# Product 1 of the last two chunks by seven half-size products throughout, with some of its activations on VectorE and three stages in a written order

## The chip, the core and the metric

The kernel runs on one core of a Trainium2 chip. The metric is the device time of one execution in microseconds (us). TensorE is called PE here, VectorE DVE, ScalarE ACT, GpSimd POOL, and SP is the engine that issues most DMAs.

## What is computed

Eight attention heads over four sequences of 768 positions, three heads ("retrieval") with a causal mask and five ("streaming") with a window of 64 positions and 4 sink positions, and behind it a two-layer block with a leaky ReLU:

```python
scores = scale * np.matmul(q, k.transpose(0, 1, 3, 2))        # (4, 8, 768, 768), head_dim 64
scores = np.where(mask, scores, -1e9)                         # causal, or window + sinks, by head
a = softmax(scores); attn = np.matmul(a, v)
x = attn.transpose(0, 2, 1, 3).reshape(3072, 512)
h = x @ w_in                                                  # product 1, 512 -> 2048
g = np.maximum(0.01 * h, h)
out = g @ w_out                                               # product 2, 2048 -> 512
```

## The kernel before

The 3072 positions are cut into eight chunks of 384 (`CH`), numbered 0 to 7; a sequence has two. For each chunk the attention gives `xts[n]`, the transposed input of product 1. Product 1 gives `g_all` (features on partitions, 16 tiles of 128 features), and product 2 takes pairs of 128-row tiles of `g_all` and writes rows of the output.

The work is software-pipelined. **Stage n** is the pass of the last loop (L1115 on) with that n: it runs product 1 of chunk n, the attention of chunk n+1 (up to stage 6) and product 2 of chunk n-1. Chunk numbers and stage numbers are the same thing in what follows. Nothing is scheduled by a tool: each engine executes its instructions in the order in which Python calls them, and semaphores hold an instruction until its inputs are there and its output buffer is free. The order is made of lists of small steps ("slots"): `Attention.slots` (a score matmul with its exponential on ACT and mask on DVE, and some slots later the product with V, "AV"), `in_slots` (product 1) and `steps` (product 2, each step half a unit of 4 matmuls of 256 columns, 14 steps for a pair). `merge` spreads one list evenly through another.

**Product 1** has two forms. A *tick* makes one tile of 128 features for the chunk: 4 matmuls of 384 columns into one PSUM bank (tag `ph`, two banks), then one leaky ReLU on ACT into `g_all` (L597, L600). A *quad* (class `Quad`) makes four such tiles by seven half-size products P1 to P7 in place of eight (sums and differences of blocks of the input, `x_sum`, and of the weights, `in_sum`, stand in for blocks). Each product is 4 matmuls of 192 columns (L686). P1, P6, P7 and P4 accumulate in one bank; after P1, P6 and P7 the running total is copied to SBUF by ACT (L700), and the next product may only start when the copy has read the bank. P2, P5 and P3 are added to those copies by DVE (L714), and each result passes the leaky ReLU on ACT (`out`, L693). Before, `BY_SEVEN` gives chunks 4, 6 and 7 two quads (features 0 to 1023) and eight ticks each.

**Product 2** uses the same trick with class `Pair`: units P1 to P7 of 8 matmuls (L800, L779), sums on DVE (L761), copies on ACT (L804) and additions on DVE (L805). Its sums of a pair are put in line by `flush` when all 16 tiles of the chunk are there.

PSUM has eight banks, two for each tag: `ph` and `psS` (scores) and `po` (AV) and `py` (product 2).

Of the kernel before, what the change touches and what calls it, by code (L numbers as in the profile page):

```python
# [11 lines left out]
FP32 = mybir.dt.float32  # L12
# [9 lines left out]
def kernel(  # L22
# [36 lines left out]
    def bank(tag, shape, dtype):  # L59
        return ps.tile(shape, dtype, name=tag, tag=tag, bufs=BANKS[tag])  # L60
# [245 lines left out]
    class Attention:  # L306
        def __init__(self, n, score_tags=("psS",), po_tags=("po", "po", "po", "po"), xt_eng="a", cross=False, xt_tag="psS"):
            self.n = n
            self.b, self.c = ORDER[n]
            self.i = self.b % 2  # L310
            xts[n] = rot.tile([128, 4, CH], BF16, name="xt", tag="xt", bufs=2)
            self.po = {}
            self.tags = score_tags
            self.po_tags = po_tags
            self.sc = 0
            self.xt_eng, self.xt_tag = xt_eng, xt_tag
            self.cross = cross
            self.sink_lo = 128 if self.c == 0 else 0
            self.units = {h: (self.retr(h) if IS_RETR[h] else self.stream(h)) for h in range(H)}
# [261 lines left out]


    done = [0] * NCH
    BY_SEVEN = {4: (0, 1), 6: (0, 1), 7: (0, 1)}

    def slab(n):
        return 4 if n % 2 else n // 2 % 2
# [1 line left out]
    def costing(us, f):  # L589
        f.us = us  # L590
        return f

    def in_slots(n, tags=("ph",)):
        def tick(t, tag=None):
            ph = bank(tag or tags[t % len(tags)], [128, 512], FP32)
            for g in range(KG):
                nc.tensor.matmul(ph[:, 0:CH], lhsT=w_in_bf[:, g, 128 * t : 128 * t + 128],  # L597
                                 rhs=xts[n][:, g, :] if n else xts[0][:, :, g, :], start=(g == 0), stop=(g == KG - 1))
            done[n] += 1
            nc.scalar.activation(out=g_all[:, slab(n) : slab(n) + 3, t, :],  # L600
                                 in_=ph[:, 0:CH].rearrange("p (j t) -> p j t", j=3), func=ACTF.Prelu, alpha=0.01)

        ks = BY_SEVEN.get(n, ())
        ticks = [costing(0.65, lambda t=t: tick(t)) for t in range(NG) if t // 4 not in ks]
        if n + 1 == NCH:
            several = [Quad(n, k, tag).slots() for k, tag in zip(ks, ("psS", "po", "ph"))]
            if len(ks) > 2:
                r = []
                for t in range(12):
                    r += [fs[t - 2 * i] for i, fs in enumerate(several) if 0 <= t - 2 * i < 8]  # L610
                    if t in (0, 1, 9, 10):
                        r.append(ticks.pop(0))
                return r
# [33 lines left out]
    def x_sums(n):  # L647
        x = xts[n].rearrange("p g (j e t) -> p g j e t", j=3, e=2)
        b = lambda a, e: x[:, KH * a : KH * a + KH, :, e, :]
        t = rot.tile([128, 4, KH, 3, 64], BF16, name="x_sum", tag="x_sum", bufs=1)  # L650
        for i, y, z in ((1, b(0, 1), b(0, 0)), (2, b(1, 1), t[:, 0]), (3, b(1, 1), b(0, 1)), (4, b(1, 0), t[:, 1])):
            nc.vector.tensor_tensor(t[:, i - 1], y, z, op=ALU.subtract)
        x_sum[n] = t
        if n + 1 == NCH:
            temps[n] = [rot.tile([128, 2, CH], FP32, name=nm, tag=tag, bufs=bufs) for nm, tag, bufs in
                        (("p1s", "kd", 2), ("us", "kd", 2), ("u3s", "kb", 1))]

    class Quad:


        def __init__(self, n, k, tag):
            self.n, self.k, self.tag = n, k, tag
            self.bank, self.late = {}, []

        def slots(self):
            return [costing(0.33, lambda u=u: self.unit(u)) for u in ("P1", "P6", "P7", "P4", "P2", "P5", "P3")] + [costing(0.0, lambda: self.late.pop()())]

        def unit(self, u):
            n, k = self.n, self.k
            while self.late:  # L670
                self.late.pop()()
# [9 lines left out]
            if first:  # L681
                self.bank[at] = bank(self.tag, [128, 512], FP32)
            s = self.bank[at]
            for m in range(2):
                for g in range(KH):
                    nc.tensor.matmul(s[:, 192 * m : 192 * m + 192], lhsT=lhs[:, g, 128 * m : 128 * m + 128], rhs=rhs[:, g],  # L686
                                     start=first and m == 0 and g == 0, stop=(g == KH - 1), skip_group_check=True)
            self.empty(u, s[:, 0:CH])

        def out(self, src, m, e):  # L690
            t = 4 * self.k + 2 * m
            dst = g_all[:, slab(self.n) : slab(self.n) + 3, t : t + 2, 64 * e : 64 * e + 64]
            nc.scalar.activation(out=dst.rearrange("p j x t -> p x j t"), in_=src.rearrange("p (x j t) -> p x j t", x=2, j=3),  # L693
                                 func=ACTF.Prelu, alpha=0.01)
            self.left -= 1
            if not self.left:
                done[self.n] += 4

        def empty(self, u, s):
            copy = lambda o: nc.scalar.activation(out=o, in_=s, func=ACTF.Copy)  # L700
            if u == "P1":
                self.left = 4
                self.p1, self.u, self.u3 = (t[:, self.k] for t in temps[n]) if n in temps and self.k < 2 else \
                    (rot.tile([128, CH], FP32, name=nm, tag=nm, bufs=1)[:] for nm in ("p1q", "uq", "u3q"))
                copy(self.p1)
            elif u == "P6":
                copy(self.u)
            elif u == "P7":
                copy(self.u3)
            elif u == "P4":  # L710
                self.out(s, 1, 0)
            else:
                t, m, e = {"P2": (self.p1, 0, 0), "P5": (self.u3, 1, 1), "P3": (self.u, 0, 1)}[u]
                nc.vector.tensor_tensor(t, s, t, op=ALU.add)  # L714
                self.late.append(lambda: self.out(t, m, e))

    def in_tile(t0, j, tag="ph", nt=4):
        ph = bank(tag, [128, 4, 128], FP32)
# [393 lines left out]
    assert not any(lists.values())  # L1112
    load_v(4)

    for n in range(2, NCH):  # L1115
        a, extra = [], ()
        if n + 2 < NCH:
# [10 lines left out]
                load_qk(n + 3, "k" if n > 2 else "kq")  # L1128
        if n + 1 < NCH:
            a = Attention(n + 1, cross=True).slots(lag=2 if n > 3 else 3)  # L1130
            a = into(a, extra) if n > 2 else a
        if n == 2:
            a = [(lambda f=f, i=(6, 9, 12, 15).index(j): (f(), in_sums(0, i + 1))) if j in (6, 9, 12, 15) else f for j, f in enumerate(a)]
        ins = in_slots(n)
        if n == 7:
            x_sums(n)
        if n == 3:
# [70 lines left out]
```

## Time and profile before

| | |
|---|---|
| runs, us | 223.74, 223.10, 221.77 (median 223.1) |
| profiled execution, us | 222.32, of which the span from first to last instruction is 220.5 |
| PE busy (matmuls) | 213.3 us, 97% of the span |
| PE weight loads busy | 169.5 us, 77% |
| DVE busy | 144.8 us, 66% |
| ACT busy | 146.8 us, 67% |
| POOL busy | 73.2 us, 33% |
| stage 5 | about 139.6 to 160.2 us of the span |
| stage 6 | about 160.2 to 188.7 us |
| stage 7 | about 188.7 to 204.6 us, then the last two pairs of product 2 to the end |

Rows of the profile name the engine, the line and the tiles (output<-input), how many there are, the busy time and the mean duration of one in ns. In a timeline the first two columns are start and duration in us. Matmuls overlap in the pipeline, so that the time a group of matmuls takes from the engine is the distance to the start of the next group, not the duration in its own row.

### The profile page before, as it was taken

Reading aid. Unit: us, or ns where it says so; the run is one execution under the profiler, and the core shown is the slowest. Engines: PE = TensorE matmul, PEld = TensorE weight load, DVE = VectorE, ACT = ScalarE, POOL = GpSimd, SP = SyncE. Lnnn points to the kernel's source line nnn. Section 1 sums busy time; section 2 is a strip of 40 time slices with the busy share of each in tenths; the row PEclk is TensorE's granted clock in tenths of the full one; section 3 lists DMA queues with packets and bytes.
Section 4 is the critical chain, followed back from the end, with each engine's and each line's share of the span. In section 5 each row is a group of like instructions: output and inputs, shape, how many; then the busy total and the mean of one; then the engine's idle time right before and its main releaser. Section 6 shows DMA issues by size and latency. Waiting matters only on the chain.

```text
span 220.5 us, 6066 instructions
## 1 busy us (share of the span) xinstructions
PE 213.3 (97%) x2436; PEld 169.5 (77%) x2436; DVE 144.8 (66%) x394; ACT 146.8 (67%) x335; POOL 73.2 (33%) x91
## 2 busy tenths in 40 slices
PE   8898999999899999999999999999999999999993
PEld 5577876668698676886688888777787888888893
DVE  6692597885989785857257875655373846626663
ACT  4767975772466997477768796687478886577220
POOL 8978472049607805305447401800000000000000
PEclk9999999999999999999999999999999999999999
DMA  9999999999999999999999994997320231200222
GB/s 130 154 173 169 188 207 188 179 153 124 152 146 230 175 135 146 155 212 117 145 206 153 139 205 99 157 137 107 81 98 5 62 86 21 95 3 0 95 109 86
DMA packets 112604, 28.79 MB, mean 131 GB/s; under 512 B 102208, under 2 KB 109632, under 8 KB 112576
## 3 DMA queue, kind: packets, MB, share of 16 engines
q0 software_dynamic: 78080, 13.37, 82.5%
q1 hardware_dynamic: 33152, 14.53, 36.2%
q10 hardware_dynamic: 1344, 0.50, 1.0%
q8 instruction: 19, 0.31, 0.7%
q14 instruction: 9, 0.07, 0.1%
HBM read 27.30 MB, written 6.29 MB: 152 GB/s over the span
## 4 chain that ended last, share of the span: by engine, by line
PE 85%; POOL 5%; DMA 4%; DVE 3%; ACT 2%; issue 1%; POOLq 0%
PE ph L597 26%; PE py L800 20%; PE po L326 7%; PE py L779 6%; PE psS L357 5%; PE ph L686 4%; DMA w_in_bf<-in_moe_w_in_dram 4%; PE psS L392 3%; PE psS L597 2%; PE po L779 2%; PE po L800 2%; POOL va L123 1%; POOL qb L116 1%; PE po L686 1%; PE psS L686 1%; ACT at L362 1%
## 5 line engine op out<-in xcount | busy, mean ns | idle before, releaser
L597 PE MATMUL ph<-xt,w_in_bf 128*128 128x384 bf16 x352 | 68.5, 326 | 0.0
L600 ACT ACTIVATE g_all<-ph 128x384 bf16<-128x384 f32 x88 | 43.2, 491 | 21.0 <-PE ph L597 18.3
L597 PEld LDWEIGHTS <-w_in_bf 128*128 128x128 bf16 x384 | 34.1, 97 | 17.3 <-issue 0.5
L362 ACT ACTIVATE at<-psS 128x384 bf16<-128x384 f32 x73 | 35.3, 495 | 8.8 <-PE psS L357 6.1
L800 PEld LDWEIGHTS <-sum 128*128 128x128 bf16 x256 | 23.8, 98 | 4.1
L116 POOL DMA_DIRECT2D kb<-in_k_dram x21 | 18.7, 911 | 20.6 <-DMA kd<-kb 18.6
L123 POOL DMA_DIRECT2D va<-in_v_dram x24 | 21.6, 920 | 0.5 <-issue 0.5
L357 PE MATMUL psS<-qd,kt 128*128 128x384 bf16 (+2 forms) x81 | 20.5, 290 | 0.1
L800 PEld LDWEIGHTS <-g_all 128*128 128x128 bf16 x192 | 18.0, 98 | 2.3
L116 POOL DMA_DIRECT2D qb<-in_q_dram x21 | 18.6, 907 | 2.7 <-DMA w_out_bf<-in_moe_w_out_dram 1.3
L326 PE MATMUL po<-va,at 128*128 128x65 bf16 x219 | 18.7, 194 | 0.0
L326 PEld LDWEIGHTS <-at 128*128 128x128 bf16 x234 | 14.7, 98 | 4.0 <-issue 0.5
L800 PE MATMUL py<-w_sum,sum 128*128 128x256 bf16 x120 | 17.7, 272 | 0.0
L397 ACT ACTIVATE ats<-psS 128x384 bf16<-128x384 f32 x33 | 15.7, 490 | 2.6 <-PE psS L392 2.0
L401 DVE TENSOR_TENSOR ats<-ats,m_win 128x384 bf16<-128x384 bf16 x35 | 12.3, 356 | 7.7 <-ACT ats L397 7.3
L761 DVE TENSOR_TENSOR sum<-g_all 128x1024 bf16<-128x1024 bf16 x24 | 16.4, 683 | 0.0
L800 PE MATMUL py<-w_out_bf,g_all 128*128 128x256 bf16 x112 | 16.1, 273 | 0.0
L800 PE MATMUL py<-w_out_bf,sum 128*128 128x256 bf16 x120 | 15.7, 273 | 0.0
L425 DVE TENSOR_TENSOR xs<-po,linv 128x384 bf16<-128x384 f32 x27 | 15.1, 558 | 0.9
L779 PEld LDWEIGHTS <-sum 128*128 128x128 bf16 x152 | 13.2, 98 | 2.2 <-issue 0.5
L264 DVE COPY kt<-kd 64x512 bf16<-64x512 bf16 x36 | 12.9, 366 | 1.3 <-DMA kd<-kb 0.9
L805 DVE TENSOR_TENSOR o<-py,u 128x256 f32<-128x256 f32 x15 | 6.3, 422 | 8.6 <-PE py L800 5.4
(249 smaller groups left out, 415.5 us busy)
## 6 DMA issues: line engine op xcount, KB each, us to landing
out_dram<-o SPq DMA_DIRECT2D x23, 256.0 KB, 3.9
va<-in_v_dram POOLq DMA_DIRECT2D x24, 128.0 KB, 7.2
qb<-in_q_dram POOLq DMA_DIRECT2D x21, 128.0 KB, 6.8
kb<-in_k_dram POOLq DMA_DIRECT2D x21, 128.0 KB, 6.3
w_out_bf<-in_moe_w_out_dram POOLq DMA_DIRECT2D x4, 512.0 KB, 12.0
w_in_bf<-in_moe_w_in_dram POOLq DMA_DIRECT2D x2, 512.0 KB, 8.7
w_in_bf<-in_moe_w_in_dram POOLq DMA_DIRECT2D x4, 256.0 KB, 7.7
vb<-va SPq DMA_DIRECT2D x6, 170.6 KB, 3.4
```

The lines of the kernel that those rows point to most:

```text
L116: nc.gpsimd.dma_start(out=t[:, g], in_=nat[nm][b, c, :, :, g])
L123: nc.gpsimd.dma_start(out=va[b][:, 3 * c + g, :, 0:D], in_=nat["v"][b, c, :, :, g])
L326: nc.tensor.matmul(o, lhsT=lhsT, rhs=rhs, start=first, stop=False, skip_group_check=True)
L357: nc.tensor.matmul(s[:, off : off + w], lhsT=kt[i][hh][:, p, 128 * kj : 128 * kj + 128], rhs=q_of(n, p, lo, CH), start=(j == 0), stop=(j = ...
L362: nc.scalar.activation(out=a[:, 0:off], in_=s[:, 0:off], func=ACTF.Exp, scale=SM)
L397: nc.scalar.activation(out=av_, in_=s[:, 0:CH].rearrange("p (j e f) -> p j e f", j=3, e=2), func=ACTF.Exp, scale=SM)
L425: nc.vector.tensor_tensor(xs[:], po[:, :, :, 0:D], linv.to_broadcast([128, 3, 2, D]), op=ALU.mult)
L597: nc.tensor.matmul(ph[:, 0:CH], lhsT=w_in_bf[:, g, 128 * t : 128 * t + 128], rhs=xts[n][:, g, :] if n else xts[0][:, :, g, :], start=(g == ...
L600: nc.scalar.activation(out=g_all[:, slab(n) : slab(n) + 3, t, :], in_=ph[:, 0:CH].rearrange("p (j t) -> p j t", j=3), func=ACTF.Prelu, alp ...
L761: nc.vector.tensor_tensor(self.s[i], x, y, op=op)
L779: nc.tensor.matmul(s[:, 0 : c1 - c0], lhsT=lhs[:, j, :], rhs=rhs[:, j, c0:c1], start=first and j == 0, stop=(j == NH - 1), skip_group_chec ...
L800: nc.tensor.matmul(s, lhsT=lhs[:, j, :], rhs=rhs[:, j, :], start=u in ("P1", "P2", "P5") and j == 0, stop=(j == NH - 1), skip_group_check= ...
```

## The change

Chunks 6 and 7 get four quads each and no ticks. Stages 5, 6 and 7 no longer merge lists: a string per stage (`WOVEN`) names the list from which each next step is taken: `p` a step of product 2, `a` a slot of attention, `t` a tick, `A` to `D` the steps of the four quads (seven products, then a last one that only puts the outstanding leaky ReLU in line), `x` the four sums of the input, `e` a copy of transposed keys, `I` one of four new weight sums (for features 1024 to 2047), `v` a transfer of shifted values.

In a woven quad the products come in the order P1, P2, P6, P5, P7, P4, P3; P2, P5 and P3 use one bank of another tag (`SIDE`: `ph` in stage 6, `po` in stage 7), and P5 is added after P7 has been copied. The copies of a quad lie in one tile with two halves (`s0` to `s3`), so that P7's copy takes the place of P1's and has to wait for the leaky ReLU that reads it. `OUTS` names, for the 16 leaky ReLUs of each chunk, those that DVE does (`v`: 9 of chunk 6, 5 of chunk 7), each as two `scalar_tensor_tensor` of 192 elements per partition.

```diff
-    BY_SEVEN = {4: (0, 1), 6: (0, 1), 7: (0, 1)}
+    BY_SEVEN = {4: (0, 1), 6: (0, 1, 2, 3), 7: (0, 1, 2, 3)}
+    SIDE = {5: 'po', 6: 'ph', 7: 'po'}
+    OUTS = {6: 'vvavvvaavaavvvaa', 7: 'vaaavaavaaaavaav'}
+    WOVEN = {
+        5: "IptatattapatpaaeetaatepaIpaapttatpattIatvtppppeIeettppp",
+        6: "pxpAaAappAaaAAapApAaBpBBaAaBBaapBpBaapCpCaCaBCpCpaaCpaaCDapaDaDppaaDDpppDDpppCDppppp",
+        7: "pxpBABApCABpABApBApApBBDCCpDCDCADBpDpCDCDCpDppp",
+    }
...
+        if n in WOVEN:
+            return {"t": ticks, **{"ABCD"[j]: Quad(n, k, ("psS" if j < 2 else "ph") if n + 1 == NCH else "ph", True).slots() for j, k in enumerate(ks)}}
...
-        if n + 1 == NCH:
-            temps[n] = [rot.tile([128, 2, CH], FP32, name=nm, tag=tag, bufs=bufs) for nm, tag, bufs in
-                        (("p1s", "kd", 2), ("us", "kd", 2), ("u3s", "kb", 1))]
+        if n in (6, 7) and len(BY_SEVEN[n]) > 0:
+            parts = [rot.tile([128, 2, CH], FP32, name=nm, tag=tag, bufs=bufs) for nm, tag, bufs in
+                     (("s0", "kd", 2), ("s1", "kd", 2), ("s2", "kb", 1), ("s3", "qb", 1))]
+            temps[n] = [[t[:, x] for x in range(2)] for t in parts]
...
+        ORDERS = (("P1", "P6", "P7", "P4", "P2", "P5", "P3"), ("P1", "P2", "P6", "P5", "P7", "P4", "P3"))
...
+            if u == "P5" and self.woven:
+                self.bank[at] = self.bank["a"]
+            elif first:
+                self.bank[at] = bank(SIDE[n] if u == "P2" and self.woven else self.tag, [128, 512], FP32)
...
-            nc.scalar.activation(out=dst.rearrange("p j x t -> p x j t"), in_=src.rearrange("p (x j t) -> p x j t", x=2, j=3),
-                                 func=ACTF.Prelu, alpha=0.01)
+            dst, src = dst.rearrange("p j x t -> p x j t"), src.rearrange("p (x j t) -> p x j t", x=2, j=3)
+            if OUTS.get(self.n, "")[4 * self.k - self.left + 4:][:1] == "v":
+                for x in range(2):
+                    nc.vector.scalar_tensor_tensor(dst[:, x], src[:, x], 0.01, src[:, x], op0=ALU.mult, op1=ALU.max)
+            else:
+                nc.scalar.activation(out=dst, in_=src, func=ACTF.Prelu, alpha=0.01)
...
+    in_sums_left = [lambda i=i: in_sums(1, i + 1) for i in range(4)]
...
+        if n in WOVEN:
+            lists = {"a": a, "p": outs, "x": [lambda: x_sums(n)], "e": [], "v": [lambda: v_shift(n + 2)], **ins}
...
+            for c in WOVEN[n]:
+                lists[c].pop(0)()
```

What this does to the order shows best on DVE and ACT. First DVE at the head of stage 6, before; names are output<-input, `x_sum` and `sum` are the sums for products 1 and 2, `o` rows of the output, `at` and `ats` masked exponentials, `xs` the attention's result:

```order
L652 TENSOR_TENSOR x_sum_3186<-xt_2835,x_sum_3186 128x384
L761 TENSOR_TENSOR sum_3209<-g_all_101 128x1024
L805 TENSOR_TENSOR o_3205<-py_3196,p1_3207 128x256
L367 TENSOR_TENSOR at_3242<-at_3242,m_caus_70 128x128
L365 TENSOR_TENSOR at_3260<-at_3260,m_caus_70 128x2x128
L401 TENSOR_TENSOR ats0_89<-ats0_89,m_win_73 128x3x2x64
L761 TENSOR_TENSOR sum_3332<-g_all_101,sum_3183 128x1024
L423 RECIPROCAL linv_3341<-po_3232 128x6
L425 TENSOR_TENSOR xs_3343<-po_3232,linv_3341 128x384
L714 TENSOR_TENSOR p1q_3224<-ph_3369,p1q_3224 128x384
```

The same place now:

```order
L661 TENSOR_TENSOR x_sum_3196<-xt_2835,x_sum_3196 128x384
L790 TENSOR_TENSOR sum_3213<-g_all_101 128x1024
L728 TENSOR_TENSOR s0_3201<-ph_3225,s0_3201 128x384
L834 TENSOR_TENSOR o_3209<-py_3191,p1_3211 128x256
L719 SCALAR_TENSOR_TENSOR g_all_101<-s0_3201 128x3x64 x2
L367 TENSOR_TENSOR at_3260<-at_3260,m_caus_70 128x128
L728 TENSOR_TENSOR s0_3201<-ph_3225,s0_3201 128x384
L365 TENSOR_TENSOR at_3278<-at_3278,m_caus_70 128x2x128
L719 SCALAR_TENSOR_TENSOR g_all_101<-s0_3201 128x3x64 x2
L728 TENSOR_TENSOR s0_3201<-ph_3225,s0_3201 128x384
L401 TENSOR_TENSOR ats0_89<-ats0_89,m_win_73 128x3x2x64
L728 TENSOR_TENSOR s1_3202<-ph_3330,s1_3202 128x384
```

The first quad's three additions (L728, L714 before) and two of its leaky ReLUs (L719) now stand among the first masks of the stage; before, the first addition of a quad came behind the first `xs`.

Second, ACT in the middle of stage 7, before (L600 a tick's leaky ReLU, L693 leaky ReLUs of quads, L804 copies of product 2):

```order
L693 ACTIVATE g_all_101<-psS_3749 128x2x3x64
L693 ACTIVATE g_all_101<-po_3755 128x2x3x64
L600 ACTIVATE g_all_101<-ph_3822 128x3x128
L804 ACTIVATE u_3832<-py_3727 128x256
L600 ACTIVATE g_all_101<-ph_3846 128x3x128
L693 ACTIVATE g_all_101<-p1s_3724 128x2x3x64 x2
L600 ACTIVATE g_all_101<-ph_3870 128x3x128
L693 ACTIVATE g_all_101<-u3s_3726 128x2x3x64
```

And now, around the place where quad A (copies in `s0`) goes from P7 to P4 (L738 copies and L721 leaky ReLUs of quads, L833 copies of product 2):

```order
L738 ACTIVATE s0_3771<-psS_3791 128x384
L738 ACTIVATE s1_3772<-psS_3785 128x384
L721 ACTIVATE g_all_101<-s0_3771 128x2x3x64
L721 ACTIVATE g_all_101<-psS_3791 128x2x3x64
L833 ACTIVATE u_3872<-py_3760 128x256
L721 ACTIVATE g_all_101<-s1_3772 128x2x3x64
L721 ACTIVATE g_all_101<-psS_3785 128x2x3x64
L738 ACTIVATE s3_3774<-ph_3894 128x384
L721 ACTIVATE g_all_101<-s2_3773 128x2x3x64
```

The ticks' leaky ReLUs that stood between the rows of two quads are gone; rows of four quads (`s0` to `s3`) follow each other, and the first two here free the banks in which quads A and B go on with P4.

More of the change, by code (lines that the diff above doesn't have):

```diff
@@ L680, in unit @@
             first = u in ("P1", "P2", "P5")
-            if first:
-                self.bank[at] = bank(self.tag, [128, 512], FP32)
+            if u == "P5" and self.woven:
+                self.bank[at] = self.bank["a"]
+            elif first:
+                self.bank[at] = bank(SIDE[n] if u == "P2" and self.woven else self.tag, [128, 512], FP32)
             s = self.bank[at]
@@ L697, in out, with add @@
                 done[self.n] += 4
+        def add(self, u, s):
+            t, m, e = {"P2": (self.p1, 0, 0), "P5": (self.u3, 1, 1), "P3": (self.u, 0, 1)}[u]
+            nc.vector.tensor_tensor(t, s, t, op=ALU.add)
+            self.late.append(lambda: self.out(t, m, e))
         def empty(self, u, s):
-            copy = lambda o: nc.scalar.activation(out=o, in_=s, func=ACTF.Copy)
             if u == "P1":
                 self.left = 4
[L703 to L710, printed above, removed]
+                self.p1, self.u, *u3 = temps[n][self.k] if (n := self.n) in temps else \
+                    [rot.tile([128, CH], FP32, name=nm, tag=nm, bufs=1)[:] for nm in self.parts()]
+                self.u3 = u3[0] if u3 else self.p1
+            if u in ("P1", "P6", "P7"):
+                nc.scalar.activation(out={"P1": self.p1, "P6": self.u, "P7": self.u3}[u], in_=s, func=ACTF.Copy)
+            if u == "P4":
                 self.out(s, 1, 0)
[L712 to L715, printed above, removed]
+            elif u == "P7" and self.woven:
+                self.add("P5", self.bank["x"][:, 0:CH])
+            elif u in ("P2", "P3") or u == "P5" and not self.woven:
+                self.add(u, s)
     def in_tile(t0, j, tag="ph", nt=4):
@@ L1130 @@
             a = Attention(n + 1, cross=True).slots(lag=2 if n > 3 else 3)
-            a = into(a, extra) if n > 2 else a
+            a = into(a, extra) if n > 2 and n not in WOVEN else a
         if n == 2:
@@ L1134 @@
         ins = in_slots(n)
+        if n in WOVEN:
+            lists = {"a": a, "p": outs, "x": [lambda: x_sums(n)], "e": [], "v": [lambda: v_shift(n + 2)], **ins}
+            if n > 2:
+                lists["e"] += extra
+            if n == 4:
+                lists["v"] = [lambda: turn_dma(7, "k")]
+            if n in (5, 6):
+                lists["I"] = in_sums_left
+            for c in WOVEN[n]:
+                lists[c].pop(0)()
+            assert not any(lists[c] for c in "aptABCDe" if c in lists) and (n < 6 or not in_sums_left)
+            if n in (3, 4):
+                nc.gpsimd.tensor_copy(hold[0:1, :], xts[n + 1][0:1, 3, 0:1])
+                load_qk(n + 3, "q")
+                load_v(n + 3)
+            outs = [f for k in range(3 * n // 2, 3 * n // 2 + 1 + n % 2) for f in steps(k)]
+            continue
         if n == 7:
```

16 lines of the change are left out of this document (11 added, 5 removed).

## The prediction

> **What bounds the kernel now.** I read the page's totals first, then the busy time by stretches, then the timeline of PE in the stages that change.
>
> ```profile
> span 220.5 us, 6066 instructions
> PE 213.3 (97%) x2436; PEld 169.5 (77%) x2436; DVE 144.8 (66%) x394; ACT 146.8 (67%) x335; POOL 73.2 (33%) x91
> ...
> PEclk9999999999999999999999999999999999999999
> ...
> 139.60:160.20 20.60, 20.60 (x223) 15.27 (x221) 11.01 (x33) 14.10 (x32) 2.77 (x4) 1.00 1.13 119
> ...
> 160.20:188.40 28.20, 28.20 (x339) 23.71 (x338) 17.28 (x44) 21.80 (x51) 0.00 (x0) 1.00 0.18 53
> 188.40:204.30 15.90, 15.90 (x146) 13.21 (x144) 8.06 (x18) 10.97 (x26) 0.00 (x0) 1.00 0.09 34
> ```
>
> The last three rows are stages 5, 6 and 7: length, then busy time of PE, of weight loads, of DVE, ACT and POOL, then the clock. In each, PE's busy time equals the length (20.60 of 20.60, 28.20 of 28.20, 15.90 of 15.90) at full clock. So PE never stands still there, and its matmuls set the time. Two things follow. Time falls only by what PE has less to do; and a new order of steps can win nothing in these stages, it can only lose, by making PE wait.
>
> **What PE saves.** How long a group keeps PE is read from starts, here in stage 7:
>
> ```profile
> 193.08 0.81 PE L597 MATMUL ph<-xt,w_in_bf 128*128 128x384 bf16 x4
> 193.73 0.49 PE L686 MATMUL psS<-x_sum,in_sum 128*128 128x192 bf16 x4
> 194.06 0.49 PE L686 MATMUL po<-x_sum,in_sum 128*128 128x192 bf16 x4
> 194.39 0.81 PE L597 MATMUL ph<-xt,w_in_bf 128*128 128x384 bf16 x4
> 195.04 0.60 PE L800 MATMUL py<-w_sum,sum 128*128 128x256 bf16 x4
> ```
>
> A tick takes 0.65 us (193.08 to 193.73, and 194.39 to 195.04), one product of a quad 0.33 us (193.73 to 194.06 to 194.39). Four ticks are 4 x 0.65 = 2.60; the quad in their place is 7 x 0.33 = 2.31. Each exchange saves 0.29 us; two are made in stage 6 and two in stage 7: **4 x 0.29 = 1.16 us**, 0.58 in each. Stage 5 keeps 16 ticks, 14 steps of product 2 and its attention: 0. What lies ahead of stage 5 and behind stage 7 is untouched. A quad has 28 weight loads against the ticks' 16, so 48 more in all.
>
> ```profile
> 190.07 0.76 PEld L686 LDWEIGHTS <-w_in_bf 128*128 128x128 bf16 x8
> ...
> L686 PEld LDWEIGHTS <-in_sum 128*128 128x128 bf16 x96 | 8.2, 97 | 1.0
> ```
>
> They cost nothing in my sum: one load lasts 97 ns, but stage 6 has 338 of them in 28.20 us, 83 ns apiece on average with three other kinds of matmul between, so loads overlap each other; and the eight products in a row at 190.07 kept their 0.33 us per four.
>
> **What the other engines must then do in time.** The bank of P1, P6, P7, P4 is handed from PE to ACT and back between every two of them. Its price stands in stage 3, where four ticks in a row share two banks:
>
> ```profile
> 106.78 2.85 PE L597 MATMUL ph<-xt,w_in_bf 128*128 128x384 bf16 x16
> 109.47 1.04 PE L800 MATMUL py<-w_out_bf,sum 128*128 128x256 bf16 x8
> ...
> 107.63 0.49 ACT L600 ACTIVATE g_all<-ph 128x384 bf16<-128x384 f32 x1 [0.40 <-PE ph L597]
> ```
>
> The first tick's matmuls are through at 106.78 + 0.65 = 107.43; ACT starts at 107.63, 0.20 later, and takes 0.49. The group needs 2.69 (106.78 to 109.47) and not 2.60: two handovers with 0.65 of other work between cost 0.045 each. So a handover to ACT needs 0.65 + 0.045, about **0.69 us** of other PE work, and nothing is lost above that. For DVE:
>
> ```profile
> 183.57 0.56 DVE L425 TENSOR_TENSOR xs<-po,linv 128x384 bf16<-128x384 f32 x1
> 184.05 0.55 DVE L714 TENSOR_TENSOR p1q<-ph,p1q 128x384 f32<-128x384 f32 x1
> 184.51 0.55 DVE L714 TENSOR_TENSOR u3q<-ph,u3q 128x384 f32<-128x384 f32 x1
> 184.98 0.68 DVE L761 TENSOR_TENSOR sum<-g_all,sum 128x1024 bf16<-128x1024 bf16 x1
> ...
> 184.63 0.53 ACT L693 ACTIVATE g_all<-p1q 128x384 bf16<-128x384 f32 x1
> ```
>
> An addition takes 0.55, so its handover needs about 0.20 + 0.55 + 0.03 = **0.78** (0.03 from its end at 184.60 to the ACT row that waits for it, 184.63). Back to back such operations follow each 0.47 us (184.05 to 184.51 to 184.98).
>
> I counted the PE work between the two ends of each handover in the new strings, with 0.33 for a product, 0.44 for a step of product 2, 0.165 for a score matmul of 384 columns and 0.09 for an AV of three. The shortest: stage 6, quad A, P7 to P4 ("AapA"): 0.165 + 0.09 + 0.44 = 0.69, against 0.69 needed. Stage 7, A's P7 to P4 ("ApBA") and D's P7 to P4 ("DpCD"): 0.44 + 0.33 = 0.77 against 0.69. Stage 6, quad C, P2 to P5 ("CaCaC"): 0.17 + 0.09, 0.33, 0.17 + 0.09, together 0.86 against 0.78. The quads' other handovers have 0.9 or more, but for two of ACT with 0.77 and 0.84. In stage 5 no pair of ticks has less than 0.81. **If ACT and DVE are free at that moment, nothing is lost.** ACT is: it loses 16 leaky ReLUs of ticks, gains 12 copies and 16 leaky ReLUs of quads and gives 14 of all to DVE, 2 fewer in the sum.
>
> DVE is the question. It gets 3 additions for each added quad, and 28 half leaky ReLUs. This operation (two inputs, multiply and maximum, 192 elements of f32) is in no row of before. The nearest:
>
> ```profile
> L974 DVE SCALAR_TENSOR_TENSOR m_one<-diff,m_caus x1: 225/225/225, 1.8 to 1.8; 128x64 bf16<-128x64 bf16 x1
> ...
> L837 DVE TENSOR_TENSOR o<-py,u 128x128 f32<-128x128 f32 x2 | 0.6, 288 | 0.0
> ...
> L805 DVE TENSOR_TENSOR o<-py,u 128x256 f32<-128x256 f32 x15 | 6.3, 422 | 8.6 <-PE py L800 5.4 <-ACT g_all L600 2.6 <-ACT g_all L693 0.7
> ...
> L714 DVE TENSOR_TENSOR p1q<-ph,p1q 128x384 f32<-128x384 f32 x4 | 2.2, 552 | 2.2 <-PE ph L686 2.2
> ...
> L643 DVE TENSOR_TENSOR in_sum<-w_in_bf 128x1024 bf16<-128x1024 bf16 x2 | 1.4, 684 | 0.0
> ```
>
> The same operation on 64 elements took 225 ns, f32 additions of 128, 256 and 384 took 288, 422 and 552. Ends: 0.225 and 0.552. I take the middle between the rows of 128 and 256, 0.355 us, and 0.275 from start to start when back to back (0.08 less, as 0.55 goes to 0.47). Then:
> - Stage 5: four weight sums of 0.684 (L643): 11.01 + 2.74 = 13.75 us in 20.60. Room.
> - Stage 6: 17.28 + 6 x 0.47 + 18 x 0.275 = 25.05 us in 28.20 - 0.58 = 27.62, 91%.
> - Stage 7: 8.06 + 6 x 0.47 + 10 x 0.275 = 13.63 us in 15.90 - 0.58 = 15.32, 89%.
>
> With 0.552 (0.47 back to back) it would be 28.56 in stage 6 and 15.58 in stage 7, more than the stages have; with 0.225, 22.7 and 12.3.
>
> DVE's order is fixed, so a queue nine tenths full is late here and there. I followed DVE's order by hand through both stages with these durations. Where P5 or P3 waits for an addition, or a copy waits for a leaky ReLU that still reads its half tile, the operation was done 0.05 to 0.3 us before PE needed it, at some twelve places by 0.2 or less; none came out late. As twelve so narrow places will not all hold, I charge **0.30 us** (0.025 each), with bounds of 0 and of 3.2 (below).
>
> Moved, and costing nothing: the transfer of shifted values and the DMA transposes of the attention's result still go out some 5.5 us of PE work ahead of the next stage (in stage 5 "tvtpppp" to "ppp" stand behind the last attention slot), as before; stores on SP follow their steps; POOL has nothing in stages 6 and 7 (0.00). If that cover were gone, PE would wait for the transposes at the head of stage 6 or 7.
>
> **Sum.** -1.16 + 0.30 = -0.86 us. The profiled execution took 222.32 us, 220.5 of them span and 1.82 around it: 221.46. The median of the runs is 223.1, 0.78 above that execution: **222.2 us**, 0.4% less.
>
> **Rivals.**
> - *The saving is eaten.* Each of the twelve narrow places is late by 0.1 us, and 1.2 us come back: 223.1. For it: DVE at 91%, and a handover with 0.69 for 0.69. Against it: once PE has waited at one place, the next ones have that much more room.
> - *DVE's leaky ReLUs hold the banks: slower.* In each of the eight quads one addition finds a pair of leaky ReLUs in front of it; the pair takes 0.55, the room is about 0.15, PE loses 0.4 each time: 8 x 0.4 = 3.2 us, net +2.0: 225.1. It decides from the point where such a pair costs more than the room, thus with an operation of 0.552, where DVE has more to do than the stage is long. For it: that end of the bound. Against it: in the new order most additions stand ahead of the pair, and the 64-element row is far below.
> - *The weight loads bind.* If loads went one after another at 97 ns, a quad would take 28 x 0.097 = 2.72 and not 2.31, 0.12 more than the four ticks: 4 x 0.12 = +0.5 us, and with the 0.30 charged above 223.9. Against it: 338 loads in 28.20 us, above.
> - *More than the sum.* There is no idle PE time to win. Only the spread of the runs (221.77 to 223.74) could show it.
>
> The Trainium skill ("Perfetto Trace Analysis", Identifying the Most-Contended Engine) holds that matmul occupancy is a poor measure of how near PE is to its limit and that the share of weight loads should be read with it. By that rule PE's 77% would leave room and fewer columns would not help while more loads might hurt, which is the third rival; the trace here disagrees, since products of 192 columns run at 0.33 us per four and ticks of 384 at 0.65.
>
> That the change does not do what it says can be left aside: the new order has 28 leaky ReLUs on DVE and no tick in stages 6 and 7.
>
> **How the numbers follow.** One per cent, about 2.2 us, is what a measurement of this kernel can tell from no change. Forecast 0.62, eaten 0.20, slower 0.10, loads 0.03, more than the sum or an outlying median 0.05. Faster by over 1% means under 220.9: 0.05. Slower by over 1% means over 225.3: about 0.07, the upper half of the slower rival and a little of the others. Within 1%: 0.88. The forecast itself lies between 221.9 (no stall) and 222.9; with the medians' spread of half a per cent on either side, and reaching to the eaten saving and part of the slower rival, the range is 220.8 to 224.5.
>
> **What would show it.** Right: stages 6 and 7 each about 0.4 to 0.6 us shorter, PE still busy all along, the half leaky ReLU near 0.355, stage 5 as long as before. Wrong: rows in the list of waits where PE waits for DVE (L728) or ACT (L738) by more than 0.3 us in total; a half leaky ReLU above 0.45; PE waiting for transposes at the head of a stage.

## The result, and the profile after

| | before | after |
|---|---|---|
| median of 16 runs each, us | 223.02 (221.77 to 225.82) | 221.38 (220.05 to 222.12) |
| ratio, with its 95% interval | | 0.9924 [0.9898, 0.9949] |
| profiled execution, us | 222.32 | 221.45 |

The change makes the kernel 0.8% faster by this measurement, 1.6 us; run a second time it came out at 0.4% (below). First the totals of the page after, then the row of the half leaky ReLUs (least, median and greatest duration in ns, first and last start):

```profile
span 219.7 us, 6221 instructions
...
PE 212.5 (97%) x2484; PEld 172.8 (79%) x2484; DVE 160.0 (73%) x438; ACT 145.0 (66%) x333; POOL 73.0 (33%) x91
```

```profile
L719 DVE SCALAR_TENSOR_TENSOR g_all<-s x28: 347/352/359, 164.3 to 203.5; 128x192 bf16<-128x192 f32 x28
```

PE has 48 matmuls more and is busy 0.8 us less; DVE is busy 15 us more. The operation that no row of before showed takes 352 ns.

To compare stages I cut both executions at the same instructions: in each stage the first `py<-w_sum,g_all` step of product 2, which opens it. The rows give stage 5, stage 6, stage 7 and the rest: length, then busy time of PE, weight loads, DVE, ACT and POOL (with the number of instructions), the granted clock of PE (1.00 is full), and two columns on DMAs. Before:

```profile
138.91:159.37 20.46, 20.46 (x222) 15.15 (x220) 10.87 (x32) 14.10 (x32) 3.46 (x4) 1.00 1.16 122
159.37:187.84 28.47, 28.47 (x342) 23.95 (x340) 17.55 (x43) 21.80 (x51) 0.00 (x0) 1.00 0.18 53
187.84:203.77 15.93, 15.93 (x146) 13.23 (x144) 8.10 (x17) 10.97 (x26) 0.00 (x0) 1.00 0.09 34
203.77:220.50 16.73, 13.30 (x138) 11.95 (x135) 8.76 (x19) 2.69 (x7) 0.00 (x0) 1.00 0.27 96
```

After:

```profile
139.21:159.86 20.65, 20.63 (x221) 15.20 (x219) 13.32 (x36) 13.60 (x32) 3.46 (x4) 1.00 1.00 116
159.86:187.82 27.96, 27.96 (x365) 25.51 (x363) 24.87 (x68) 20.29 (x49) 0.00 (x0) 1.00 0.20 57
187.82:203.17 15.35, 15.35 (x170) 14.72 (x168) 13.41 (x31) 11.06 (x27) 0.00 (x0) 1.00 0.10 36
203.17:219.70 16.53, 13.31 (x138) 11.95 (x135) 9.25 (x22) 2.80 (x8) 0.00 (x0) 1.00 0.27 96
```

Stage 6 is 0.51 us shorter, stage 7 0.58, stage 5 is 0.19 longer, the rest 0.20 shorter. Stage 5 starts 0.30 later. The sum, 0.30 + 0.19 - 0.51 - 0.58 - 0.20 = -0.80, is the difference of the spans, 220.5 to 219.7.

**Where 0.19 us went in stage 5.** PE looks busy there too (20.63 of 20.65). The loss shows only in the starts, in the timeline after:

```profile
147.47 0.87 ACT L397 ACTIVATE ats<-psS 128x384 bf16<-128x384 f32 x2
147.83 0.58 DVE L264 COPY kt<-kd 64x512 bf16<-64x512 bf16 x2
...
148.44 0.63 DVE L401 TENSOR_TENSOR ats<-ats,m_win 128x384 bf16<-128x384 bf16 x2
148.50 0.34 PE L392 MATMUL psS<-qd,kt 128*128 128x64 bf16 x6
148.86 0.24 PE L326 MATMUL po<-va,ats 128*128 128x65 bf16 x2
```

The six score matmuls at 148.50 need about 0.16 us (six times 64 columns, as many as one matmul of 384 has, and a tick's four take 0.65), but the next group of PE starts 0.36 later: 0.20 us lost. It multiplies V with `ats`, whose masks on DVE (L401) start only at 148.44, behind two key copies (L264). The first of the two exponentials was through at about 147.96.

**Where 0.07 us went in stage 6.** It is 0.51 shorter and not 0.58. The narrowest place of my list, quad A's P7 to P4 with 0.69 us of other work for a handover of 0.69, reads:

```profile
165.13 0.26 PE L326 MATMUL po<-va,at 128*128 128x65 bf16 x3
165.22 0.60 PE L829 MATMUL py<-w_sum,sum 128*128 128x256 bf16 x4
165.71 0.49 PE L709 MATMUL ph<-x_sum,w_in_bf 128*128 128x192 bf16 x4
...
165.16 0.49 ACT L738 ACTIVATE s<-ph 128x384 f32<-128x384 f32 x1
```

The step of product 2 at 165.22 keeps PE 0.49 and not 0.44: P4 waited by 0.05 for the copy, which ends at 165.65. PE had gone from P7 to the next group at 164.97, so this handover took 0.74 (0.19 to ACT's start, 0.49 for the copy, 0.06 back to PE) and not 0.69. The rest of the 0.07 stands in one more place: the product at 167.83 keeps PE 0.36 and not 0.33, where the next product on the bank waits for a copy (167.65 to 168.14). Both are copies on ACT; no addition and no leaky ReLU of DVE shows up in the starts.

### The profile page after: what moved, and what is told of

It reads as the page before. It is cut to its first block, busy times and chain, and to the rows that moved or that the text cites. A ratio compares the mean times of both kernels' runs of the same rounds, so it can differ in the third digit from the quotient of the medians.

```text
span 219.7 us, 6221 instructions
## 1 busy us (share of the span) xinstructions
PE 212.5 (97%) x2484; PEld 172.8 (79%) x2484; DVE 160.0 (73%) x438; ACT 145.0 (66%) x333; POOL 73.0 (33%) x91
## 4 chain that ended last, share of the span: by engine, by line
PE 58%; DMA 24%; POOL 8%; issue 6%; DVE 1%; SPq 1%; ACT 1%; POOLq 0%
PE py L829 20%; PE ph L604 12%; DMA kd<-kb 9%; PE ph L709 7%; DMA kb<-in_k_dram 6%; DMA w_out_bf<-in_moe_w_out_dram 6%; PE po L326 5%; DMA w_in_bf<-in_moe_w_in_dram 4%; PE psS L357 3%; POOL va L123 2%; PE po L709 2%; POOL kb L116 2%; PE py L808 2%; PE po L829 2%; PE psS L392 2%
## 5 line engine op out<-in xcount | busy, mean ns | idle before, releaser
L604 PE MATMUL ph<-xt,w_in_bf 128*128 128x384 bf16 x288 | 55.5, 326 | 0.0
L607 ACT ACTIVATE g_all<-ph 128x384 bf16<-128x384 f32 x72 | 35.3, 490 | 19.1 <-PE ph L604 16.2
L604 PEld LDWEIGHTS <-w_in_bf 128*128 128x128 bf16 x320 | 28.6, 97 | 15.3 <-issue 0.5
L362 ACT ACTIVATE at<-psS 128x384 bf16<-128x384 f32 x73 | 34.6, 496 | 8.0 <-PE psS L357 5.8
L401 DVE TENSOR_TENSOR ats<-ats,m_win 128x384 bf16<-128x384 bf16 x35 | 12.8, 375 | 6.3 <-ACT ats L397 5.6
L829 PE MATMUL py<-w_out_bf,sum 128*128 128x256 bf16 x120 | 16.2, 272 | 0.0
L264 DVE COPY kt<-kd 64x512 bf16<-64x512 bf16 x36 | 11.4, 322 | 4.7 <-DMA kd<-kb 4.3
L326 PEld LDWEIGHTS <-ats 128*128 128x128 bf16 x210 | 10.1, 97 | 3.6 <-DVE ats L401 1.7
```

Source lines behind the costliest of these rows:

```text
L326: nc.tensor.matmul(o, lhsT=lhsT, rhs=rhs, start=first, stop=False, skip_group_check=True)
L362: nc.scalar.activation(out=a[:, 0:off], in_=s[:, 0:off], func=ACTF.Exp, scale=SM)
L829: nc.tensor.matmul(s, lhsT=lhs[:, j, :], rhs=rhs[:, j, :], start=u in ("P1", "P2", "P5") and j == 0, stop=(j == NH - 1), skip_group_check= ...
```

## The experiments

The timed medians move by more than the effect, so each run is read by its stages, cut at the same instructions. The lengths repeat within 0.01 to 0.02 us between two profiles of one kernel, as the first two runs show.

### The kernel before against itself, and the change once more

No edit in either. 

> The kernel before, run against itself: what a difference of nothing looks like. The stages' lengths of the profiled execution (between the first P4 step of product 2 in each stage) should repeat: stage 5 20.46, stage 6 28.47, stage 7 15.93 us within 0.1, since PE is busy all along there. What differs from run to run should lie ahead of stage 5, where transfers are awaited. Theory A (the timed 1.64 us of the change are the 1.16 of PE time and half a microsecond of run-to-run spread): medians of the two copies can differ by 0.3 to 0.5 us. Theory B (all of the 1.64 us is the change): they agree within 0.2 us.

```profile
139.25:159.70 20.45, 20.45 (x221) 15.14 (x219) 10.86 (x32) 14.10 (x32) 3.47 (x4) 1.00 1.01 122
159.70:188.17 28.47, 28.47 (x341) 23.95 (x339) 17.55 (x43) 21.80 (x51) 0.00 (x0) 1.00 0.18 53
188.17:204.11 15.94, 15.94 (x147) 13.23 (x145) 8.09 (x17) 10.97 (x26) 0.00 (x0) 1.00 0.09 34
```

Ratio 0.9999 [0.9964, 1.0035]; medians 222.25 and 222.43 us. They agree within 0.2 us, which by itself was theory B's sign; but the median of the same kernel was 223.02 in the first comparison, 0.6 to 0.8 above both. The stages repeat as expected.

> The changed kernel once more. Theory A (PE does 1.16 us less; some 0.2 are lost in stage 5; the rest of the timed difference is spread): stage 6 27.9 to 28.0 us, stage 7 15.35, stage 5 20.6, and a timed gain nearer to 1.0 to 1.3 us than to 1.6. Theory B (the order of the steps also gains, outside of the two stages): the timed gain is again 1.5 us or more, and the profile shows a stretch outside of stages 6 and 7 that is shorter by 0.4 us or more.

```profile
139.61:160.26 20.65, 20.63 (x221) 15.19 (x219) 13.31 (x36) 13.62 (x32) 3.46 (x4) 1.00 0.99 116
160.26:188.22 27.96, 27.96 (x365) 25.50 (x363) 24.87 (x68) 20.30 (x49) 0.00 (x0) 1.00 0.20 57
188.22:203.57 15.35, 15.35 (x170) 14.72 (x168) 13.41 (x31) 11.07 (x27) 0.00 (x0) 1.00 0.10 36
```

Ratio 0.9961 [0.9926, 0.9997]: 221.57 against 222.43, 0.86 us. The stages repeat to the last digit or the one before it, -0.90 us in sum, as in the first comparison; the timed gain went from 1.64 to 0.86.

Theory B falls: the gain is not 1.5 us again, and no stretch outside of stages 6 and 7 gained 0.4. Theory A has the stages right; the timed 0.86 lies below its 1.0 to 1.3. From the start of stage 5 to the end of the span it is 81.59 and 81.65 us in the two profiles of before, 80.49 in both of after (with spans given to 0.1 us): -1.10 to -1.16, the stages' -0.90 and 0.2 to 0.25 at the very end. That last part lies behind all computation: from the end of DVE's last addition to the end of the span it is 3.15 to 3.26 us in the three profiles with the old order (the next run is the third), and 2.83 to 2.87 in all nine with the new one, the run without the exchange among them. Why stays open.

What spreads the times lies mostly ahead of stage 5. Its start, the left column, is 138.91, 139.25, 139.21 and 139.61 in these four profiles, and between 137.26 and 140.09 in those below. The chain of waits of the repeated run shows what this early part hangs on (start, us, what):

```profile
23.18 12.55 DMA w_out_bf<-in_moe_w_out_dram
...
69.55 7.11 DMA kb<-in_k_dram
77.96 9.45 DMA kd<-kb
```

### Four matmuls fewer in each of stages 6 and 7

```diff
-            for g in range(KG):
+            last = KG - 1 - (n > 5 and 8 <= t < 12)
+            for g in range(last + 1):
```

> The kernel before with the last of the four matmuls left out in four ticks each of stages 6 and 7 (part of product 1 isn't computed): 8 x 0.1625 = 1.30 us of PE work less, and nothing else changed in order, weight sums, engines or buffers. Theory A (PE time alone sets the end): 1.30 us faster, 0.65 in each stage, by the stages' lengths; timed 1.0 to 1.6. Rival (what came of the change is from its order or from the relief of ACT): the cut gives clearly less than 1.30, since ACT still has all leaky ReLUs and must empty a bank after 0.49 us in place of 0.65.

```profile
159.67:187.49 27.82, 27.82 (x337) 23.56 (x335) 17.55 (x43) 21.77 (x51) 0.00 (x0) 1.00 0.19 54
187.49:202.78 15.29, 15.29 (x143) 12.83 (x141) 8.09 (x17) 10.86 (x26) 0.00 (x0) 1.00 0.10 35
```

Stage 6 is 0.65 us shorter than before, stage 7 0.64: 1.29 of 1.30. Timed 220.96 against 222.43, ratio 0.9946 [0.9912, 0.9981]. PE's work is what sets these stages, one for one, and nothing else in the old order stood right behind it. The run can't tell columns from weight loads, since each matmul left out takes its load with it. The changed kernel can: its stage 7 has 24 loads more and is shorter by the whole 0.58 of the columns.

### The written order without the exchange

```diff
-    BY_SEVEN = {4: (0, 1), 6: (0, 1, 2, 3), 7: (0, 1, 2, 3)}
+    BY_SEVEN = {4: (0, 1), 6: (0, 1), 7: (0, 1)}
...
-        6: "pxpAaAappAaaAAapApAaBpBBaAaBBaapBpBaapCpCaCaBCpCpaaCpaaCDapaDaDppaaDDpppDDpppCDppppp",
+        6: "pxpAaAappAaaAAapApAaBpBBaAaBBaapBpBaaptpataBptpaapaattapaatppaatppptpppppppp",
-        7: "pxpBABApCABpABApBApApBBDCCpDCDCADBpDpCDCDCpDppp",
+        7: "pxpBABAptABpABApBApApBBttpttABptpttpppp",
```

> The changed kernel's written orders, banks, products' order and VectorE leaky ReLUs, but with quads 2 and 3 of chunks 6 and 7 computed by ticks again (16 matmuls of 384 columns each, their places where some of the quads' products stood). Theory A: PE has all of its old work, so stages 6 and 7 are no shorter than before (28.5 and 15.9 us or up to 0.3 more where ticks stand close), stage 5 about 0.2 longer as in the changed kernel; timed 0 to 0.5 us slower than before. Theory B (the written order itself gains): stages 6 and 7 or the time come out 0.4 us or more below before.

```profile
138.40:159.05 20.65, 20.63 (x221) 15.20 (x219) 13.31 (x36) 13.61 (x32) 3.46 (x4) 1.00 0.98 116
159.05:187.99 28.94, 28.93 (x341) 24.06 (x339) 20.13 (x54) 19.84 (x47) 0.00 (x0) 1.00 0.19 55
187.99:203.92 15.93, 15.93 (x146) 13.23 (x144) 9.70 (x23) 9.93 (x23) 0.00 (x0) 1.00 0.09 34
```

Timed 222.89 against 222.43, ratio 1.0025 [0.9992, 1.0057]. Stage 7 is as before, stage 5 has its 0.20 us, and stage 6 is 0.47 longer, more than the 0.3 I had allowed: most of it at three places between 177.7 and 180.8, where my string has too little between scores and AVs. So theory B falls here too: the new order by itself wins nothing in the three stages, and all that is gained in them is the exchange's. (The second halves of the two strings had to be written anew for the ticks, so this is not the changed kernel's order throughout.) Here PE is again busy 28.93 of 28.94 us; the waits hide in the durations of its rows:

```profile
180.23 0.25 PE L326 MATMUL po<-va,at 128*128 128x65 bf16 x3
180.50 0.34 PE L392 MATMUL psS<-qd,kt 128*128 128x64 bf16 x6
```

Three AV matmuls take 0.09 elsewhere (165.13 to 165.22 above), here the next group starts 0.27 later.

### All leaky ReLUs on ScalarE

```diff
-    OUTS = {6: 'vvavvvaavaavvvaa', 7: 'vaaavaavaaaavaav'}
+    OUTS = {}
```

> The changed kernel with all leaky ReLUs of the quads on ScalarE again: 14 more there (9 in stage 6, 5 in stage 7), 28 half ones fewer on VectorE. ScalarE's busy time becomes about 20.3 + 9 x 0.45 = 24.3 us of stage 6's 27.96, and 11.1 + 5 x 0.45 = 13.3 of stage 7's 15.35; VectorE's falls to 19.9 and 10.7. Theory A (PE's work sets the time, VectorE's leaky ReLUs only give ScalarE room for its bank copies): the copies of P1, P6 and P7 come late at the places with 0.69 to 0.77 us of room, stages 6 and 7 together 0.2 to 1.0 us longer than in the changed kernel. Rival (VectorE's leaky ReLUs hold up additions and banks): the stages get shorter than in the changed kernel, by what is lost there now (0.07 us in stage 6).

```profile
158.32:188.21 29.89, 29.09 (x365) 25.63 (x363) 20.30 (x50) 23.64 (x58) 0.00 (x0) 1.00 0.18 53
188.21:204.25 16.04, 15.72 (x171) 14.75 (x168) 11.21 (x23) 12.54 (x31) 0.00 (x0) 1.00 0.09 34
```

Theory A has the direction, not the size: stage 6 is 1.93 us longer than in the changed kernel, stage 7 0.69, together 2.62 where I had expected 0.2 to 1.0. Against the kernel before, stage 6 is 1.42 us longer and stage 7 0.11: more than the gain is gone. (The one execution took 222.51 us beside 222.42 of the kernel before; its stage 5 began at 137.68, earlier than in any profile of before.) ACT is busy 23.64 of 29.89 us, 79%, and still late. Its timeline in stage 6, with the waiting row of PE at the end:

```profile
168.95 0.48 ACT L340 ACTIVATE at_sink<-psS 128x384 bf16<-128x384 f32 x1
...
169.32 0.52 ACT L721 ACTIVATE g_all<-s 128x384 bf16<-128x384 f32 x1
...
169.73 0.49 ACT L362 ACTIVATE at<-psS 128x384 bf16<-128x384 f32 x1
170.10 0.50 ACT L738 ACTIVATE s<-ph 128x384 f32<-128x384 f32 x1
170.27 0.32 PE L357 MATMUL psS<-qd,kt 128*128 128x384 bf16 x1 [0.38 <-ACT at L362]
```

Four operations stand one behind another, a leaky ReLU among them, and the next score has no bank until the exponential at 169.73 has read it. I had counted the copies alone as late; here it is an exponential, behind a leaky ReLU.

### The half leaky ReLUs twice

```diff
-                for x in range(2):
+                for x in (0, 1, 0, 1):
                     nc.vector.scalar_tensor_tensor(dst[:, x], src[:, x], 0.01, src[:, x], op0=ALU.mult, op1=ALU.max)
```

> The changed kernel with each half leaky ReLU of VectorE done twice into the same place (28 operations more, nothing else): VectorE gets 18 x 0.275 = 4.95 us more in stage 6 and 2.75 in stage 7, thus 24.87 + 4.95 = 29.8 for 27.96 us and 13.41 + 2.75 = 16.2 for 15.35. It is the slower rival's case, made on purpose. Theory A (the room on VectorE decides; below a full queue a late operation costs little): stage 6 at least 1.9 us longer, stage 7 at least 0.8, and waits of PE for VectorE appear. If a pair's own length were what counts (each pair ahead of an addition costs 0.4 us, whatever the load), 8 quads x 0.8 = 6 us or more would be added. If VectorE's work is not awaited at all: no change.

```profile
160.13:191.03 30.90, 29.30 (x365) 25.33 (x363) 29.07 (x87) 20.44 (x49) 0.00 (x0) 1.00 0.18 52
191.03:206.95 15.92, 15.51 (x168) 14.72 (x168) 15.10 (x39) 11.24 (x27) 0.00 (x0) 1.00 0.09 34
```

```profile
173.82 1.15 DVE L719 SCALAR_TENSOR_TENSOR g_all<-s 128x192 bf16<-128x192 f32 x4
...
174.90 0.55 DVE L728 TENSOR_TENSOR s<-ph,s 128x384 f32<-128x384 f32 x1
...
175.50 0.49 PE L709 MATMUL ph<-xt,w_in_bf 128*128 128x192 bf16 x4 [0.63 <-DVE s L728]
```

Stage 6 is 2.94 us longer than in the changed kernel, stage 7 0.57 (I had expected at least 0.8; eight of the ten added operations lie in it, 39 rows of DVE for 31). This is the slower rival's mechanism, word for word: an addition behind leaky ReLUs, and PE behind the addition. But it takes a DVE that is busy 29.07 of 30.90 us, 94%, with groups of four in front of one addition; it cost 3.5 us, and no sum of 6. At 89% (24.87 of 27.96) and with pairs nothing of it is seen. The run raises the load and the length of the group together, so it can't say which of the two brings the waits.

### Stage 5's masks

The first try moves three key copies by four steps, the second behind the third mask:

```diff
-        5: "IptatattapatpaaeetaatepaIpaapttatpattIatvtppppeIeettppp",
+        5: "IptatattapatpaataateeepaIpaapttatpattIatvtppppeIeettppp",
```

> The changed kernel with three key copies of stage 5 (VectorE, 0.28 us each) issued four steps later, behind the two masks of the streaming heads that PE waits for at 148.50. Theory A (these copies, standing ahead of the masks in VectorE's queue, are the whole of stage 5's 0.20 us): stage 5 is 20.46 us again, as in the kernel before, stages 6 and 7 stay 27.96 and 15.35. Rival (the four weight sums that stage 5 now has make VectorE late anyway): the wait moves to the next mask, and stage 5 keeps 0.1 to 0.2 us of it.

```profile
137.26:158.04 20.78, 20.63 (x221) 15.10 (x219) 13.48 (x36) 13.60 (x32) 3.46 (x4) 1.00 0.99 115
```

Theory A fails: the wait moved to the next mask, as the rival said, but stage 5 lost 0.32 us, more than the rival's 0.1 to 0.2, and what stands ahead of that mask is the three copies and an addition (0.41 us at 147.50), not a weight sum. DVE's timeline, with the row of PE that waits:

```profile
146.70 0.88 DVE L264 COPY kt<-kd 64x512 bf16<-64x512 bf16 x3
...
147.84 0.34 DVE L401 TENSOR_TENSOR ats<-ats,m_win 128x384 bf16<-128x384 bf16 x1
...
148.23 0.23 PE L326 MATMUL po<-va,ats 128*128 128x65 bf16 x2 [0.15 <-DVE ats L401]
```

(This one execution took 219.63 us, the least of all, and only because its stage 5 began at 137.26.)

```diff
-        5: "IptatattapatpaaeetaatepaIpaapttatpattIatvtppppeIeettppp",
+        5: "IptatattapatpaataatpaIpaapeettaetpattIatvtppppeIeettppp",
```

> The changed kernel with the same three key copies of stage 5 moved further, behind the third mask in a row, which waited for them in the run before this one (three copies of 0.88 us and an addition of 0.41 stood ahead of it). Theory A (what PE loses in stage 5 is VectorE's order around these three masks, not its load): stage 5 is 20.46 us, stages 6 and 7 stay 27.96 and 15.35; PE has then the 1.16 us less of the sum but for 0.07, and the time is 0.9 to 1.2 us below the kernel before, 0.2 below the changed one. Rival (VectorE's load of 13.3 us with the four weight sums makes some mask late wherever the copies stand): stage 5 keeps 0.1 to 0.3 us.

```profile
140.09:160.54 20.45, 20.45 (x221) 15.13 (x219) 13.56 (x36) 13.60 (x32) 3.46 (x4) 1.00 1.01 117
160.54:188.50 27.96, 27.96 (x365) 25.48 (x363) 24.87 (x68) 20.28 (x49) 0.00 (x0) 1.00 0.20 57
188.50:203.86 15.36, 15.36 (x171) 14.73 (x169) 13.42 (x31) 11.07 (x27) 0.00 (x0) 1.00 0.10 36
```

Stage 5 is 20.45 us again, with the four weight sums and a DVE as busy as in the changed kernel (13.56 us against 13.32). So it was the order around three masks, not the load. Timed 221.48 against 222.83, ratio 0.9917 [0.9885, 0.9950]. By its stages this version is 1.09 us faster than the kernel before (0.01 + 0.51 + 0.57) and 0.2 faster than the changed one, a difference that the timing of medians can't show.

### Two more quads, in stage 5

The second copies of quad 1 lie in a tile that key copies have left (two copies per quad, as elsewhere in the new order). The edit of the first try, then the second string:

```diff
-    BY_SEVEN = {4: (0, 1), 6: (0, 1, 2, 3), 7: (0, 1, 2, 3)}
+    BY_SEVEN = {4: (0, 1), 5: (0, 1), 6: (0, 1, 2, 3), 7: (0, 1, 2, 3)}
...
-        5: "IptatattapatpaaeetaatepaIpaapttatpattIatvtppppeIeettppp",
+        5: "IptatatpapatpaapaateeepaIpaaptatptIaaxeeveBABAIpABpABApBApABBpAB",
...
+        5: "IptatatxapatpaataatpaIpaapeettaepaIaeeevBABApABpABApBApApBBABpIp",
```

> The same exchange once more: two of the four quads of chunk 5 by seven products, too, in a new written order of stage 5 (8 ticks among the attention, the two quads behind it, the key copies late as in the run with copies moved). PE saves 2 x 0.29 = 0.58 us more; VectorE gets four differences of the input (1.65 us) and 6 additions. Theory A (each exchange gives its 0.29 us of PE time as long as ScalarE and VectorE keep up): stage 5 from 20.65 to 19.9 to 20.2 us. Rival (the denser attention, with fewer ticks to cover the exponentials and masks, makes PE wait): stage 5 at 20.6 us or longer.

Stages 5 and 6 took 20.83 and 30.48 us, 2.7 more than in the changed kernel. Two rows of PE's timeline:

```profile
157.27 0.82 PE L712 MATMUL po<-x_sum,in_sum 128*128 128x192 bf16 x8 [1.12 <-DVE p1q L731]
...
162.62 0.61 PE L832 MATMUL py<-w_out_bf,g_all 128*128 128x256 bf16 x4 [0.89 <-ACT g_all L724]
```

Additions of P2 came late behind the input's differences and the key copies, and product 2 of the same chunk asked for leaky ReLUs that were not done.

> Two quads of chunk 5 once more, with what held them up the first time moved: the four differences of the input go out in the first third of the stage, the key copies lie ahead of the quads, and the quads end two steps of product 2 ahead of the next stage. Theory A (the first try lost its 0.58 us because VectorE's differences and copies, 2.3 us, stood ahead of P2's additions, and because leaky ReLUs came after stage 6's first step of product 2 asked for them): the waits of 1.29 us in the quads and of 1.06 at the head of stage 6 shrink to under 0.3 each; stages 5 and 6 together 47.9 to 48.6 us, against 48.61 in the changed kernel. Rival (with 8 ticks fewer the stage lacks cover for its attention and its banks): they stay above 48.9.

```profile
139.09:160.42 21.33, 20.57 (x246) 16.67 (x244) 16.78 (x45) 14.77 (x36) 3.46 (x4) 1.00 0.98 117
160.42:189.56 29.14, 28.42 (x365) 25.36 (x364) 25.49 (x68) 21.33 (x51) 0.00 (x0) 1.00 0.18 51
...
152.65 0.24 PE L326 MATMUL po<-va,ats 128*128 128x65 bf16 x2 [0.56 <-DVE ats L401]
```

50.47 us for both, above the 48.9 of the rival. The waits that I had aimed at are no longer listed, others came in their place. The last row is one of them: the AV at 152.65 waits for a mask that DVE starts at 152.23, when ACT's exponential is through. Its scores started at 151.13, and PE had only one step of product 2 and two AVs to put behind them. This fits the rival, that half as many ticks beside the attention cover too little of it; that it is the whole of the loss is not shown, since stage 6 lost 1.18 us as well. I did not pursue it.

## Why the prediction held, step by step

- **The forecast of 222.2 us** (220.8 to 224.5, 0.4% faster, within 1% most likely) held: 221.38, and 221.57 in the second comparison, both somewhat under the forecast's own 221.9 to 222.9. The kernel before was itself at 222.43 in the second; the change came out as 0.76% [0.51, 1.02] and 0.39% [0.03, 0.74], the forecast's 0.4% at the one and outside the other. The first comparison's 1.64 us is nearly twice the forecast's 0.86, and the second's 0.86 is just that; the stage lengths are the same in both, and the kernel before alone came out 0.59 apart (223.02 and 222.43). That the profiled execution came to 221.45, beside 221.46 of the sum, is luck: it includes a start of stage 5 that was 0.30 later, and an end that was 0.20 shorter, neither of them in the sum.
- **PE's 1.16 us.** Shown: cutting 1.30 us of matmuls gave 1.29, the order without the exchange gained nothing in the three stages, and stage 7 is shorter by just 0.58, stage 6 by 0.51.
- **The 0.30 charged for twelve narrow places** was too much for them. They cost 0.07 in all, 0.05 of it at the one place that I had listed as the narrowest. I had charged it for a late DVE; both places wait for copies on ACT, and the handover that I had put at 0.69 took 0.74. The list of waits, which I had named as the sign of being wrong, could not have shown this: the profile lists no wait of PE at all between 139 and 204 us, though 0.20 and 0.07 were lost there.
- **Stage 5 at nothing** was the step that failed, by 0.20 us. I reasoned from its load: 13.75 us of DVE in 20.60, "room". The load was about right (13.32), the conclusion was not. I had followed DVE's order by hand only in the two full stages, and not in the one with a third of its time free, where the new string put copies ahead of masks. The two errors, 0.23 and 0.20, nearly cancel: -0.90 in place of -0.86.
- **"PE never stands still there"** was right for the old order but for 0.09 us (in stage 5 a tick that starts at 141.25 is followed at 141.99, after 0.74 and not 0.65; stage 6 has the like at 165.53). Both stand ahead of scores against the sinks, and the changed kernel has them too. But the row I took it from can't show it: 20.63 of 20.65 and 28.93 of 28.94 us were "busy" in stages that lost 0.20 and 0.47. The starts show it.
- **The half leaky ReLU**, bounded by 0.225 and 0.552 and taken at 0.355 us, takes 0.352. That the middle came so close is luck: the lower row was of 64 elements of bf16 with other operators, the upper ones were additions that read PSUM. DVE's load came out at 24.87 and 13.41 us for 25.05 and 13.63.
- **The slower rival** is a real mechanism, shown by doubling the operation, and lies above this kernel's load. I had put its decision point at a queue that is fuller than the stage is long, and the doubled run (29.8 us of work for 27.96) lies beyond it. Where between the two loads the waits set in was not measured.
- **The weight loads** did not bind. Loads are now busy 14.72 of stage 7's 15.35 us, 96%, up from 13.23 of 15.93, and the stage is shorter by the full saving. The rule of the Trainium skill that I weighed ("Perfetto Trace Analysis", Identifying the Most-Contended Engine) names MFU, the matmul work done as a share of the peak, beside the share of weight loads; I had read the loads' share alone. Read alone it does not fit this kernel: 77% would have told of room, and yet in stage 7 fewer columns with more loads gave the whole 0.58.
- **What I had left unpriced**: ScalarE. I had said that ACT is free, since it does 2 operations fewer in the sum. It is free only because DVE takes 14 leaky ReLUs; without that, stages 6 and 7 are 1.53 us longer than in the kernel before (2.62 us given back for 1.09 gained).

## What to carry to other kernels

Where an engine sets the time of a stage, price an exchange by its own start-to-start times and expect it one for one, and then look for its cost in the order of the engines that follow, row by row, in every stage whose order is rewritten, above all in those with "room". An engine that is busy 65% of a stage can still be late at three operations in a row. When an effect is smaller than the spread of the runs, compare stretches between the same two instructions: here they repeat within 0.02 us between profiles while whole runs of one kernel differ by 2 to 4.

## What was not expected of the hardware

- A profile's busy PE hides waits of up to 0.2 us per group, because a matmul's modelled end reaches past its start-to-start time: six score matmuls are shown with 0.34 us, whether the next group follows after 0.17 or after 0.36.
- An ACT that is 79% busy (23.64 of 29.89 us) cost 1.9 us in stage 6, a DVE that is 89% busy (24.87 of 27.96) nothing that the starts show: the 0.07 of that stage stands behind copies on ACT, there 73% busy (20.29 of 27.96). So the share alone did not tell; in the rows shown several operations stood behind one another on the late engine just when PE needed the last of them. Stage 5's masks show it for DVE, late and in time with nearly the same load (13.48 and 13.56 us); for ACT no run has changed the order and kept the load.
- The spread of the runs, 2 to 4 us, sits mostly ahead of stage 5, whose start differed by up to 2.8 us between profiles (137.26 to 140.09), and where transfers stand in the chain of waits. How large a part of it each transfer has was not measured.
